# Moving the sums of gate blocks, the decay of the states and the products of decays from VectorE to GpSimd

## The chip, the cores and the metric

The kernel runs on one core of a Trainium2 chip. The metric is the device time of one execution in microseconds (us). A core has a matrix engine (TensorE, PE in the profile; its weight loads are PEld), a vector engine (VectorE, DVE), an activation engine (ScalarE, ACT), GpSimd (POOL), and a queue engine that only issues transfers (SyncE, SP). Each works through its own queue in order, and semaphores tie the queues together. Operands lie in SBUF (128 partitions); matmul results land in PSUM.

## What is computed

A gated linear recurrence over 768 tokens for 4 x 8 heads of 48 dimensions, followed by a two-layer network with a per-channel leaky activation, on 3072 tokens:

```python
f = 1.0 / (1.0 + np.exp(-f_logit))
for t in range(S):
    state = f[:, :, t, :, None] * state + np.einsum('bhd,bhe->bhde', k[:, :, t], v[:, :, t])
    y[:, :, t] = np.einsum('bhd,bhde->bhe', q[:, :, t], state)
...
x = attn_out.transpose(0, 2, 1, 3).reshape(B * S, H * D)     # 3072 x 384
h = x @ w_in                                                 # 384 x 2048
g = np.maximum(h, 0.0) + alpha * np.minimum(h, 0.0)
return g @ w_out                                             # 2048 x 384
```

Everything is float32.

## The kernel before

The recurrence is worked in chunks. A step handles two batch rows and 128 tokens; there are 12 steps (`steps`, L726), which alternate between the two pairs of batch rows, so that a step continues the state of the step two before it. Each step has four stages, written as generators that give up control after each piece: `prepare` (P, L258), `carry` (O, L432), `attend` (S, L506) and `network` (n, L609). The string `USUAL` (L37) lays out by hand in which order the pieces of neighbouring steps are issued; the order holds for TensorE, VectorE and ScalarE (L734). For GpSimd's and SyncE's queues there is no hand-written order: the framework's scheduler places their instructions by when their inputs and buffers are ready, and every queue then runs in the order that was built. In the steady state one period holds the recurrence of step n, the preparation of step n+1 and the network of step n-1.

`prepare` loads `f`, `q`, `k` and `v` (L266, L276; from step 1 on by GpSimd's queue), applies the sigmoid (L279) and forms products of gates: scans over 32-token blocks (`ps` L317, `ss` L319), scaled queries and keys (`us` L321, L330; `k4` L347; `kh`, `ks` L374, L398; `q3` L368, L406). Near its end it forms `f64`, the decay of the state over a half-chunk of 64 tokens, as a product of two entries of the scan `ps` (L414: four small multiplications of 48 x 8 elements in a middle step, whose input and output lie on different partitions).

`carry` makes the matmuls between blocks (`off`) and the new contribution to the state (`pd`, L484). The state lives in the free rows of the tile `vs`, beside the values. `moved(0)` at the end of `carry` and `moved(1)` in the last piece of `attend` bring it forward over a half-chunk: first the old state times `f64` (L494, 48 x 768), into the rows on the other side of the tile, then two additions of `pd` from PSUM (L498). `py` (L574) is the matmul that reads state and values; its result `y` is laid out as the network's input `xT` by ten transfers from the SP, ScalarE and GpSimd queues (L603).

`network` makes eight blocks of hidden units (`ph`, L618; 48 matmul calls into PSUM banks of a pool of four). ScalarE takes the negative part (L623), VectorE combines it to `gate` (L625). The second layer is not multiplied directly: it is done in seven block products instead of eight (`product`, L655 to L687), which needs four sums and differences of blocks of `gate`, the tile `S`, made by `sums` (L693) after the fourth and after the eighth `ph` block, 128 x 512 elements each. Of these S[1] needs S[0], and S[3] needs S[1]. The products run in the order `pa`, `pb`, then `pc` (reads S[1]), `pd` (S[0]), `pa` again, `pc` again (S[2]) and `pe` (S[3]). VectorE's additions after them (`plus`, L661) combine the results and so free the PSUM banks for the next network's `ph`. The first step's network is plain and has no sums, so 11 networks have them.

Of the kernel before, what the change touches and what calls it, by code (L numbers as in the profile page):

```python
# [15 lines left out]
ALU = mybir.AluOpType  # L16
# [5 lines left out]
U = 2  # L22
# [36 lines left out]
def kernel(  # L59
# [30 lines left out]
    nc = tc.nc  # L90
    B, NC, _, HP, _ = qT.shape
    DM = v.shape[-1]
    H = 2 * HP
    D = DM // H
# [27 lines left out]
    def pair(name):  # L122
        return psa.tile([128, 2, 512], F32, tag="pair", name=name)
# [124 lines left out]
    def rows(par):  # L248
        return slice(64 * par, 64 * par + D)
# [4 lines left out]
    def halves(cc):  # L254

        return slice(CH * cc, CH * cc + CH), slice(CH * (1 - cc), CH * (1 - cc) + D)

    def prepare(bp, c, x):  # L258
# [150 lines left out]
        f64 = x["f64"] = work.tile([128, U, H], F32, tag="f64", name=f"f64_{i}")  # L409
        by64 = pre.rearrange("p (a c j) i -> p a c j i", c=NC2, j=2)  # L410
        for cc in range(0 if c else 1, NC2 if c < NC - 1 else 1):
            for par in range(2):
                g64 = by64[rows(par), :, cc, :, NB]
                nc.vector.tensor_tensor(f64[halves(cc)[1], :, par:H:2].rearrange("p u h -> p (u h)"),  # L414
                                        g64[:, :, 0], g64[:, :, 1], ALU.mult)
        yield
        for cc in range(0 if c else 1, NC2):
# [14 lines left out]
    def carry(bp, c, x):  # L432

        i = f"{bp}_{c}"
        q3, ks, kh, f64 = (x[n] for n in ("q3", "ks", "kh", "f64"))
        off = pair(f"off_{i}")
        for u in range(U):
            for hp in range(HP):
                for cc in range(NC2):
                    g = (u * HP + hp) * NC2 + cc  # L440
                    o = (u * HP + hp) * DB
                    for par in range(2):
                        r_ = rows(par)
                        nc.tensor.matmul(off[CH * cc:CH * cc + DB, par, o:o + DB],  # L444
                                         lhsT=kh[r_, g], rhs=q3[r_, g, 2], start=True, stop=True)
        if not c:
            for u in range(U):
                for hp in range(HP):
                    for j in range(NJ):
                        g = (u * HP + hp) * NJ + j  # L450
                        o = U * HP * DB + (u * HP + hp) * 16
                        for par in range(2):
                            r_ = rows(par)
                            nc.tensor.matmul(off[DB * j:DB * (j + 1), par, o:o + 16], lhsT=x["k16"][r_, g],
                                             rhs=x["q16"][r_, g], start=True, stop=True)
            for u in range(U):
                o = U * HP * DB + u * HP * 16
                nc.scalar.copy(ad[:, u, :, :, 16:DB], off[:, :, o:o + HP * 16].rearrange("p r (h t) -> p r h t", h=HP))
        for cc in range(NC2):
            s_ = slice(CH * cc, CH * cc + DB)  # L460
            for par in range(2):
                nc.scalar.copy(A[s_, :, par * HP:(par + 1) * HP, CH * cc + DB:CH * (cc + 1)],
                               off[s_, par, 0:U * HP * DB].rearrange("p (u h t) -> p u h t", u=U, h=HP))


        if not c:
            pk = pair(f"pk_{i}")
            for u in range(U):
                for hp in range(HP):
                    a = (u * HP + hp) * NC2  # L470
                    nc.tensor.transpose(pk[:, u, hp * 128:(hp + 1) * 128], ks[:, a:a + 2].rearrange("p c s t -> p (c s t)"), ident)
            ksn = x["ksn"] = work.tile([128, U, HP * 128], F32, tag="ksn", name=f"ksn_{i}", bufs=1)
            for u in range(U):
                nc.scalar.copy(ksn[:, u], pk[:, u])
        yield
        pd = pair(f"pd_{i}")
        ksn = x["ksn"]
        for u in range(U):
            for hp in range(HP):
                for cc in range(NC2):  # L480
                    for par in range(2):
                        o = (u * HP + hp) * D
                        s_ = halves(cc)[0]
                        nc.tensor.matmul(pd[rows(par), cc, o:o + D],  # L484
                                         lhsT=ksn[s_, u, hp * 128 + 64 * par:hp * 128 + 64 * par + D],
                                         rhs=vs[bp][s_, cc, u, (2 * hp + par) * D:(2 * hp + par + 1) * D], start=True, stop=True)

        def moved(cc):

            of, to = halves(cc)[1], halves(1 - cc)[1]  # L490
            was, then = (vs[bp][p, a, :, 0:DM].rearrange("p u (h e) -> p u h e", e=D)
                         for p, a in ((of, cc), (to, 1 - cc)))
            if c or cc:
                nc.vector.tensor_tensor(then, was, f64[of].unsqueeze(3).broadcast_to((D, U, H, D)), ALU.mult)  # L494
            for par in range(2):
                now = pd[rows(par), cc, 0:U * HP * D].rearrange("p (u h e) -> p u h e", u=U, e=D)
                if c or cc:
                    nc.vector.tensor_tensor(then[:, :, par:H:2], then[:, :, par:H:2], now, ALU.add)  # L498
                else:
                    nc.scalar.copy(then[:, :, par:H:2], now)  # L500

        x["moved"] = moved
        moved(0)
        yield

# [103 lines left out]
    def network(bp, c, x):  # L609
# [3 lines left out]
        for f in range(NH):  # L613
            ph = bank(f"ph{f}_{i}")
            tiles = (2 * f, 2 * f + 1) if plain else (f, f + NH)
            for kt in range(NK):
                for j, m in enumerate(tiles):
                    nc.tensor.matmul(ph[:, j * T:(j + 1) * T], lhsT=w_in_sb[:, kt, m * 128:(m + 1) * 128],  # L618
                                     rhs=xT[:, kt], start=(kt == 0 and j == 0), stop=(kt == NK - 1 and j == 1),
                                     skip_group_check=True)  # L620
            neg = work.tile([128, 2, T], F32, tag="neg", name=f"neg{f}_{i}")
            phv = ph.rearrange("p (j t) -> p j t", j=2)
            nc.scalar.activation(neg, phv, AF.Relu, scale=-1.0)  # L623
            for j, m in enumerate(tiles):
                nc.vector.scalar_tensor_tensor(gate[:, m % NH, m // NH], neg[:, j], om[:, m:m + 1], phv[:, j],  # L625
                                               ALU.mult, ALU.add)
            if not plain and f % 4 == 3:
                sums(slice(f - 3, f + 1))
            yield
# [63 lines left out]
    def sums(fs_):  # L693

        s = late["S"]
        u0, u1 = slice(0, C), slice(C, T)
        of = lambda j, u: gate[:, fs_, j, u]
        for to, x_, y_, op in ((s[:, 0, fs_], of(0, u1), of(1, u1), ALU.add),
                               (s[:, 1, fs_], s[:, 0, fs_], of(0, u0), ALU.subtract),
                               (s[:, 2, fs_], of(0, u0), of(0, u1), ALU.subtract),  # L700
                               (s[:, 3, fs_], of(1, u0), s[:, 1, fs_], ALU.subtract)):
            nc.vector.tensor_tensor(to, x_, y_, op)  # L702

    def halves_of_w_out():

# [28 lines left out]
    with tc.manual_schedule(engines={mybir.EngineType.PE, mybir.EngineType.DVE, mybir.EngineType.Activation}):  # L734
        for _ in range(IDLE):
            nc.tensor.matmul(idle[0:32, 0:8], lhsT=ones[:, 0:32], rhs=ones[:, 0:8], start=True, stop=True)
        run = {}
        for n, step in enumerate(steps):
            x = {}
            for key, stage_ in zip("POSn", (prepare, carry, attend, network)):  # L740
                run[key, n] = stage_(*step, x)
        for key in order:
            next(run[key] if key in run else pieces[key[0]])
# [55 lines left out]
```

## Time and profile before

| | |
|---|---|
| median of 3 runs | 622.16 us (620.33 to 623.74) |
| span of the profiled execution | 622.1 us |
| VectorE, sums L702 | 88 instructions, 60.6 us, mean 688 ns |
| VectorE, decay of the states L494 | 20 instructions, 19.1 us, mean 952 ns |
| VectorE, products of decays L414 | 40 instructions, 6.7 us, mean 168 ns |
| VectorE, additions to the states L498 | 40 instructions, 22.1 us, mean 552 ns |
| GpSimd, issuing transfers (L266, L276, L603) | 77 instructions, 49.4 us |

The profiled execution's span is that of a median run. In the profile a group of instructions is named by its line, its engine and by tiles as output<-input (`S<-gate`); `us` as a tile name is a tile, not a unit. "Busy" counts an engine's instructions from start to end; instructions that follow each other closely overlap a little, so start-to-start distances are somewhat shorter than durations. A bracket such as `[0.17 <-DVE o L661]` gives the idle time ahead of an instruction and what ended it. A wait that is ended by several engines is put down to the one that came last. TensorE is told apart as matmul (PE) and weight load (PEld). What GpSimd has to do before the change is filling tiles at the start and issuing transfers; as its queue runs in order, a transfer that waits for its buffer holds up what stands behind it.

### The profile page before, as it was taken

The page shows a single profiled execution, that of the slowest core. Times are in us where ns is not written, and L with a number is a line of the kernel's source. Part 1 is how long each engine was busy: PE and PEld are TensorE (multiplying, and loading weights), DVE is VectorE, ACT ScalarE, POOL GpSimd, SP SyncE. Part 2 cuts the span into 40 slices and gives each one's busy share as a digit, 9 for nine tenths or more (in the row PEclk, how much of TensorE's full clock was granted, in tenths as well). Part 3 has the DMA queues.
Part 4 walks back from the last instruction along what each step waited for, and adds up shares of the span by engine and source line. Part 5 has one row for each costly group of instructions (what it writes and reads, how often), then busy time and mean ns, then how long its engine had stood idle before and what let it go on. Part 6 is the DMA issues. An engine that isn't in the chain of part 4 may idle for free.

```text
span 622.1 us, 19062 instructions
## 1 busy us (share of the span) xinstructions
PE 592.1 (95%) x8212; PEld 529.8 (85%) x8212; DVE 497.1 (80%) x997; ACT 246.6 (40%) x466; POOL 63.0 (10%) x117
## 2 busy tenths in 40 slices
PE   3568999999999999999999999999999999999997
PEld 3457866898899899899899899899889889889997
DVE  7588998899898798798798798798888888762261
ACT  5677862441641272262261351352253243223110
POOL 9120010001000011001001001001001000000000
PEclk9999999999999999999999999999999999999999
DMA  9964632014404314214313313413313401201000
GB/s 290 367 234 155 190 85 52 36 36 108 98 8 96 72 35 107 67 35 95 79 35 90 84 35 88 86 36 86 87 36 85 87 3 26 53 2 27 26 0 26
DMA packets 68116, 50.43 MB, mean 81 GB/s; under 512 B 47168, under 2 KB 60608, under 8 KB 68032
## 3 DMA queue, kind: packets, MB, share of 16 engines
q1 hardware_dynamic: 56656, 25.01, 15.6%
q0 software_dynamic: 6864, 22.35, 12.7%
q10 hardware_dynamic: 4512, 1.85, 1.7%
q8 instruction: 65, 1.06, 0.7%
q14 instruction: 19, 0.16, 0.1%
HBM read 36.21 MB, written 4.72 MB: 66 GB/s over the span
## 4 chain that ended last, share of the span: by engine, by line
PE 88%; DVE 6%; ACT 3%; issue 2%; DMA 1%; ACTq 0%; DVEq 0%
PE ph L618 39%; PE pc L657 9%; PE pa L657 8%; PE pd L657 5%; PE pe L657 4%; PE pb L657 4%; PE py L574 4%; PE po L638 3%; PE raw L520 3%; PE qu L535 3%; PE pd L484 3%; PE off L444 1%; PE xt L592 1%; DVE gate L625 1%; DMA f<-in_fT 1%
## 5 line engine op out<-in xcount | busy, mean ns | idle before, releaser
L618 PE MATMUL ph<-xT,w_in_sb 128*128 128x256 f32 x1152 | 258.7, 382 | 0.7 <-DVE Csum L661 0.7
L618 PEld LDWEIGHTS ph<-xT,w_in_sb 128*128 128x128 f32 x1152 | 216.4, 190 | 33.4 <-issue 2.3
L623 ACT ACTIVATE neg<-ph 128x512 f32<-128x512 f32 x96 | 57.4, 598 | 200.8 <-PE ph L618 139.5
L625 DVE SCALAR_TENSOR_TENSOR gate<-neg,om,ph 128x256 f32<-128x256 f32 x192 | 82.7, 478 | 50.6 <-ACT neg L623 50.4
L657 PE MATMUL pc<-t,S 128*128 128x192 f32 x352 | 61.7, 329 | 0.0
L657 PE MATMUL pa<-w_out_sb,gate 128*128 128x192 f32 x352 | 61.3, 327 | 0.1
L657 PEld LDWEIGHTS pa<-w_out_sb,gate 128*128 128x128 f32 x352 | 57.9, 190 | 1.0 <-DVE gate L625 0.4
L657 PEld LDWEIGHTS pc<-t,S 128*128 128x128 f32 x352 | 57.3, 190 | 0.6
L526 DVE COPY_PREDICATED ad<-mraw,raw 128x256 f32<-128x256 int32 (+1 forms) x96 | 42.4, 442 | 11.1 <-PE raw L520 8.6
L541 DVE COPY_PREDICATED ad<-mquad,qu 128x224 f32<-128x224 int32 (+6 forms) x140 | 42.0, 300 | 6.2
L419 ACT COPY A<-q 48x512 f32<-48x512 f32 x44 | 27.2, 619 | 36.1 <-DVE q L368 35.7
L563 ACT COPY A<-ad 32x256 f32<-32x256 f32 x96 | 38.7, 403 | 1.4
L330 DVE TENSOR_TENSOR us<-us,fs 128x768 f32<-128x768 f32 (+5 forms) x60 | 36.8, 614 | 0.0
L678 ACT ACTIVATE o<-pa 128x192 f32<-128x192 f32 x11 | 3.7, 332 | 75.2 <-PE pa L657 72.3
L661 DVE SCALAR_TENSOR_TENSOR Csum<-pc,Csum 128x192 f32<-128x192 f32 x22 | 7.9, 357 | 30.3 <-PE pc L657 30.1
L287 DVE TENSOR_TENSOR qd<-qd,f 128x768 f32<-128x768 f32 (+2 forms) x36 | 27.2, 756 | 6.0 <-ACT qd L282 6.0
L520 PEld LDWEIGHTS raw<-qd,k 48*32 48x32 f32 x1536 | 18.5, 109 | 15.3 <-issue 13.1
L520 PE MATMUL raw<-qd,k 48*32 48x80 f32 x1536 | 24.0, 243 | 7.6 <-issue 4.4
L702 DVE TENSOR_TENSOR S<-gate 128x512 f32<-128x512 f32 x44 | 30.3, 688 | 0.8
L657 PE MATMUL pe<-w_out_sb,S 128*128 128x192 f32 x176 | 30.4, 326 | 0.0
L657 PE MATMUL pd<-w_out_sb,S 128*128 128x192 f32 x176 | 30.4, 326 | 0.0
L657 PE MATMUL pb<-t,gate 128*128 128x192 f32 x176 | 30.4, 326 | 0.0
(101 smaller groups left out, 758.3 us busy)
## 6 DMA issues: line engine op xcount, KB each, us to landing
w_out_raw<-in_w_out SPq DMA_DIRECT2D x8, 767.8 KB, 5.8
w_in_raw<-in_w_in SPq DMA_DIRECT2D x8, 767.2 KB, 11.9
q<-in_qT POOLq DMA_DIRECT2D x11, 512.0 KB, 4.2
f<-in_fT POOLq DMA_DIRECT2D x11, 512.0 KB, 4.5
k<-in_kT POOLq DMA_DIRECT2D x11, 512.0 KB, 4.9
out<-o SPq DMA_DIRECT2D x24, 192.0 KB, 2.7
vs<-in_v POOLq DMA_DIRECT2D x22, 192.0 KB, 4.6
ksn<-kt SPq DMA_DIRECT2D x80, 32.0 KB, 2.0
```

The costliest lines, as they stand in the source:

```text
L287: nc.vector.tensor_tensor(qdv[d], qdv[d - 1][:, :, :, 1:5 - d], f[:, :, 1:5 - d].rearrange("p (g i) r -> p g i r", i=NB), ALU.mult)
L330: nc.vector.tensor_tensor(us[:, :, UO[m]:UO[m] + 4 * n].rearrange("p g (i r) -> p g i r", r=4), us[:, :, skip:skip + 4 * n].rearrange("p g ...
L419: nc.scalar.copy(A[halves(cc)[1], :, par * HP:(par + 1) * HP, CH * cc:CH * (cc + 1)], q3[rows(par)].rearrange("p (u h c) s t -> p u h c (s ...
L520: nc.tensor.matmul(raw[DB * j:DB * (j + 1), par, hp * C:hp * C + QW], lhsT=k[r_, g * DB:(g + 1) * DB], rhs=qd[r_, g], start=True, stop=True)
L526: nc.vector.copy_predicated(adu[:, :, :, d:4], mraw[:, d, :, d:4].bitcast(I32).unsqueeze(1).broadcast_to((128, H, NB, n)), rv[:, :, QO[d]: ...
L541: nc.vector.copy_predicated(ad[:, u, :, :, 4 * m:DB], mquad[:, lo:lo + n].bitcast(I32).unsqueeze(1).unsqueeze(1).broadcast_to((128, 2, HP, ...
L563: nc.scalar.copy(A[s_, u, :, s_], ad[s_, u].rearrange("p r h t -> p (r h) t"))
L618: nc.tensor.matmul(ph[:, j * T:(j + 1) * T], lhsT=w_in_sb[:, kt, m * 128:(m + 1) * 128], rhs=xT[:, kt], start=(kt == 0 and j == 0), stop=( ...
L623: nc.scalar.activation(neg, phv, AF.Relu, scale=-1.0)
L625: nc.vector.scalar_tensor_tensor(gate[:, m % NH, m // NH], neg[:, j], om[:, m:m + 1], phv[:, j], ALU.mult, ALU.add)
L657: nc.tensor.matmul(to[:, 0:DH], lhsT=of(f), rhs=by(f), start=(f == 0 and not more), stop=(f == NH - 1), skip_group_check=True)
L702: nc.vector.tensor_tensor(to, x_, y_, op)
```

## The change

Three calls move from VectorE to GpSimd, with the same operands:

```diff
@@ prepare
             for par in range(2):
                 g64 = by64[rows(par), :, cc, :, NB]
-                nc.vector.tensor_tensor(f64[halves(cc)[1], :, par:H:2].rearrange("p u h -> p (u h)"),
+                nc.gpsimd.tensor_tensor(f64[halves(cc)[1], :, par:H:2].rearrange("p u h -> p (u h)"),
                                         g64[:, :, 0], g64[:, :, 1], ALU.mult)
@@ carry, moved
             if c or cc:
-                nc.vector.tensor_tensor(then, was, f64[of].unsqueeze(3).broadcast_to((D, U, H, D)), ALU.mult)
+                nc.gpsimd.tensor_tensor(then, was, f64[of].unsqueeze(3).broadcast_to((D, U, H, D)), ALU.mult)
@@ sums
                                (s[:, 3, fs_], of(1, u0), s[:, 1, fs_], ALU.subtract)):
-            nc.vector.tensor_tensor(to, x_, y_, op)
+            nc.gpsimd.tensor_tensor(to, x_, y_, op)
```

VectorE keeps the gates, the additions to the states and all the rest of `prepare`. GpSimd now also runs, in a middle step, eight sums, two decays and four products beside its transfers; the products feed the decays on the same engine, the decays feed VectorE's additions, and the sums feed TensorE.

## The prediction, made before the changed kernel was run

> **What bounds the kernel now.** I read the page first, then one window per step of the steady part, then VectorE's timeline at the end of one step, then the waits.
>
> ```profile
> PE 592.1 (95%) x8212; PEld 529.8 (85%) x8212; DVE 497.1 (80%) x997; ACT 246.6 (40%) x466; POOL 63.0 (10%) x117
> ...
> PE 88%; DVE 6%; ACT 3%; issue 2%; DMA 1%; ACTq 0%; DVEq 0%
> ```
>
> TensorE (PE) is busy 95% of the span and makes 88% of the chain that ended last. VectorE (DVE) is busy 80%, GpSimd (POOL) 10%. The next view cuts the span at the first `raw` matmul of each step; columns are the stretch, its length, then busy us and instructions of each engine.
>
> ```profile
> 198.12:245.80 47.68, 47.61 (x658) 43.34 (x657) 40.21 (x79) 15.68 (x33) 4.47 (x7) 1.00 0.28 66
> 293.48:341.23 47.75, 47.65 (x658) 43.40 (x657) 41.45 (x86) 17.91 (x36) 4.47 (x7) 1.00 0.28 68
> ```
>
> In a step TensorE is without work for 0.1 us or less, at full clock. So freeing VectorE can give almost nothing in the ten steps that make up the time after 150 us; it can only lose, where VectorE becomes late for TensorE. The waits say where that is nearest (columns: us in total, times, longest):
>
> ```profile
> PEld ph L618 <- DVE Csum L661: 1.0, 1, 1.0
> PEld ph L618 <- DVE o L661: 0.9, 5, 0.2
> PEld pa L657 <- DVE gate L625: 0.4, 1, 0.4
> ```
>
> At five step ends (245, 293, 341, 388 and 436 us) the first `ph` load of the next network stands 0.17 us behind VectorE's `o` additions (L661), which free the PSUM banks; at 152 us 0.98 us. There VectorE has no slack. At 484 us the additions end 0.5 us ahead of that load, at 198 us 2.2 us. VectorE's timeline into the end of one such step (start, duration):
>
> ```profile
> 227.00 0.69 DVE L702 TENSOR_TENSOR S<-gate 128x512 f32<-128x512 f32 x1
> 227.72 0.69 DVE L702 TENSOR_TENSOR S<-S,gate 128x512 f32<-128x512 f32 x1
> ...
> 229.54 0.75 DVE L317 TENSOR_TENSOR_SCAN ps<-fs,ones 128x289 f32<-128x289 f32 x1
> ...
> 235.58 0.36 DVE L661 SCALAR_TENSOR_TENSOR Csum<-pc,Csum 128x192 f32<-128x192 f32 x1 [1.52 <-PE pc L657]
> ...
> 239.56 0.95 DVE L494 TENSOR_TENSOR vs<-vs,f 48x768 f32<-48x768 f32 x1
> 240.55 1.12 DVE L498 TENSOR_TENSOR vs<-vs,pd 48x384 f32<-48x384 f32 x2
> ...
> 245.66 0.72 DVE L414 TENSOR_TENSOR f<-ps 48x8 f32<-48x8 f32 x4
> 246.41 0.36 DVE L661 SCALAR_TENSOR_TENSOR Csum<-pc,Csum 128x192 f32<-128x192 f32 x1
> ```
>
> From the second group of sums (227.00) to the last additions (247.42) VectorE stands still once, 1.52 us for `pc`. All three moved kinds of work lie in this stretch, and its length decides.
>
> **The change: what VectorE loses.** L702: 88 instructions, mean 688 ns, 60.6 us. L494: 20 of 952 ns, 19.1 us. L414: 40 of 168 ns, 6.7 us. Together 86.4 us of 497.1. In the stretch, start to start: four sums 2.54 us (227.00 to 229.54), one decay 0.99 (239.56 to 240.55), four products 0.75 (245.66 to 246.41): 4.28 us. The other halves lie elsewhere: the first group of sums and the first decay at 214 to 217.8 us, ahead of places where VectorE waits for ScalarE anyway (0.68 us before L287, 0.31 us before the last gate). Removing them is worth nothing to TensorE, which covers them.
>
> **What GpSimd gains, and its price.** The trace has no two-input operation on GpSimd. From below: its memset of 512 elements, 0.53 us. From above: its affine select of 128 elements, 0.742 us, or 5.8 ns an element, which is 3.0 us for 512. I take a fixed 0.15 us (its 4-element copies last 0.178) and twice the memset's 0.88 ns an element (1.812 us for 2048), once per input: p = 0.15 + 512 x 1.76 ns = 1.05 us for a sum, 1.5 us for a decay of 768 elements, 0.2 us for a product. It is nearer the low end because a memset streams like a tensor operation and a select computes a condition. GpSimd's own load is no bound: 8 x 1.05 + 2 x 1.5 + 4 x 0.2 = 12.2 us on top of 4.47 in a step of 47.7. The Trainium skill (GPSIMD Engine Reference, 3.1) has 4497 ns for a two-input add of 2048 elements; an estimate from it is 1.12 us for a sum, by which the stretch below would be 0.3 us longer. No run here shows it.
>
> **Do the two engines hold each other up?** The start of the trace has GpSimd copies beside VectorE operations with two SBUF inputs:
>
> ```profile
> 7.31 0.18 POOL L166 COPY mquad<-inq 128x4 f32<-128x4 f32 x1
> ...
> 7.57 0.92 POOL L174 COPY mhalf<-inq 128x8 f32<-128x8 f32 x1
> ...
> 12.16 1.03 POOL L190 COPY dense<-ident 128x48 f32<-128x48 f32 x1
> ```
>
> A copy of 4 elements takes 0.18 us while VectorE is idle. The copy of 8 begun at 7.57 ends at 8.49, as VectorE's L287 (7.49 to 8.45) ends; the one begun at 12.16 ends at 13.19, as L321 (11.91 to 13.10) ends. A GpSimd read waits for the VectorE operation under way and gets in before the next. Whether VectorE then waits for GpSimd these short copies can't show: from below nothing, from above the whole GpSimd operation. I take a hold of most of it, as exclusion seen from one side is likely to work from both. The Trainium skill (SBUF — State Buffer, Who interferes with whom) says so: VectorE with two SBUF inputs and a GpSimd operation that reads SBUF share one read interface, and the second to come is blocked until the first ends. On GpSimd's side the trace agrees (1.03 us against 0.18); by the full rule the time would be about 632 us.
>
> **The sum.** GpSimd in the stretch: 4 x 1.05 + 1.5 + 4 x 0.2 = 6.5 us. If all of it holds VectorE, which loses 4.28 us of work and can use up the 1.52 us of idleness, the additions end 6.5 - 4.28 - 1.52 = 0.7 us later. Nine turns of the hold also lose the 0.09 us by which VectorE's operations overlap (0.69 long, 0.60 apart): 0.8 more. Against this, 2.9 us of the 13.6 us of other work (L661, L498, the transpose) read PSUM or one tensor and can run beside GpSimd; they lie behind 235.58, where GpSimd has the decay and products left, 2.3 us, so a fifth of that comes back: 0.4 us. I take +1.1 us a step end. Bounds: 4.28 us less work with no hold leaves -1.7 us (worth at most the 0.17 us wait); p = 3.0 us with a full hold gives 12 + 4.4 + 0.8 - 5.8, +11 us, which I count among the less than 1 in 10 above the range since no streaming row is near it. TensorE pays in full at the six step ends without slack, 0.6 at 484 us, nothing at 198 and 531 us: 6 x 1.1 + 0.6 = 7.2 us. Ramp and tail: nothing; the last network's `pc` starts at 605.8 and its second sum would end at 602.2 + 0.2 + 2 x 1.05 = 604.5. Sum on the profiled execution's 622.1 us, which is also the median (622.16): 629.3, say **629 us**; 625 to 637 for this case alone, from 0.5 to 2.2 us a step end.
>
> **New waits and queues.** GpSimd takes its queue in order:
>
> ```profile
> 206.54 0.73 POOL L266 DMA_DIRECT2D k<-in_kT  x1 [18.45 <-PE raw L520]
> 221.31 0.73 POOL L266 DMA_DIRECT2D q<-in_qT  x1 [14.04 <-ACT qd L282]
> 232.36 0.72 POOL L266 DMA_DIRECT2D f<-in_fT  x1 [10.32 <-DVE us L321]
> 233.08 0.61 POOL L276 DMA_DIRECT2D vs<-in_v  x1
> 234.08 1.08 POOL L603 DMA_DIRECT2D xT<-y  x2 [0.40 <-ACT y L583]
> ```
>
> The sums of 214 us have 7 us ahead of `q`. Those of 227 us end about 235, with VectorE's operations between them; `s2`, the first that TensorE reads, about 230.5 against `pc` at 232.7. The `f` and `vs` loads are for two steps on. The two `xT` transfers, behind sums, products and decay, go at about 239 instead of 234 and land 4.1 us later, 243 against `ph` at 247.6: covered, with 4 us to spare. The additions L498 now wait on VectorE for GpSimd's decay; queued behind them stand the gates at 217 us, and at 240 us the end of the stretch.
>
> **The rivals.** (a) *No hold*: GpSimd fits its reads into the gaps and VectorE isn't delayed; the step ends stay where they are, 621 to 622 us. For it: the VectorE operations beside the waiting copies kept their length (L287 0.96 us, as in its mean). (b) *L498 waits*: the first decay stands behind the first sums on GpSimd, 214.1 + 4 x 1.05 + 1.5 = 219.8, so the additions end 2 us later than 218.9; 1 us of that is swallowed by the idle 0.68 + 0.31, the last gate comes 1 us late where `pa` has 0.7 us, and the hold comes on top: some 2.3 us x 9 steps, 643 us. Against it: the decay's inputs are ready near 198 us, when GpSimd is idle. (c) *Faster*: the stretch gets shorter by up to 1.7 us and the waits of TensorE for VectorE go: 1.0 + 0.9 + 0.4 above, 0.2 for L526, and 2 x 0.35 us of L414 in the ramp at 19.9 and 50.3 us, 3.2 us: 619 us. It decides if a sum holds VectorE for less than 0.5 us; against it stands that the whole pool is hardly 3 us.
>
> **How the numbers follow.** Forecast 0.50, (b) 0.15, (a) 0.26, (c) 0.09. A measurement tells about 0.5%, 3.1 us, from no change; so slower 0.65, same 0.26, faster 0.09. The range 618.5 to 643 takes in (c) and most of (b), and leaves larger prices of p out.
>
> **What would show it.** Right: L702, L494, L414 on GpSimd, sums of 1 to 1.3 us apart; L317 to L347 each begun later than the one before ended, or longer, while sums run; `Csum` after `pc` at or past its old distance; PEld `ph` waiting 1 us or more for L661 at six step ends, steps of 48.8 us instead of 47.7. Wrong: steps of 47.7 us with VectorE idle more, rival (a); waits of L498 for GpSimd, rival (b); `pc` waiting for `S` or `ph` for `xT` would show a GpSimd queue that I have ordered wrongly.

## The result, and the profile after

The changed kernel takes 632.22 us (median of 4, 630.29 to 633.9) against 621.86 us before (median of 4): a ratio of 1.0165, 95% interval 1.0136 to 1.0195. It is slower by some 10 us.

The page of the changed kernel, engines and the chain that ended last:

```profile
PE 592.1 (94%) x8212; PEld 527.7 (84%) x8212; DVE 463.0 (73%) x849; ACT 246.1 (39%) x466; POOL 254.6 (40%) x265
...
PE 68%; DVE 13%; POOL 7%; issue 5%; ACT 5%; DMA 1%; ACTq 0%; DVEq 0%
```

VectorE gave up 86.4 us of work, yet is busy only 34.1 us less: the other 52 us are its remaining operations, which got longer. GpSimd, whose operations were no part of the chain, now has 7% of it. Two steps, cut at the first `raw` matmul as before:

```profile
202.45:250.97 48.52, 47.73 (x657) 43.16 (x656) 36.66 (x70) 17.29 (x35) 21.85 (x21) 1.00 0.27 66
250.97:299.61 48.64, 47.70 (x658) 43.15 (x657) 37.68 (x72) 17.86 (x35) 21.86 (x21) 1.00 0.28 67
```

TensorE's busy time in a step is what it was, 47.7 us; the step is 0.9 us longer. The waits of its weight loads after the start show for what (us in total, times, longest):

```profile
PEld pc L657 <- POOL S L702: 7.6, 7, 1.8
...
PEld ph L618 <- DVE o L661: 1.0, 6, 0.2
PEld pc L657 <- DVE Csum L661: 1.0, 1, 1.0
```

The product `pc` waits seven times for the sums on GpSimd. The wait for L661 at the step ends, which the forecast saw growing to more than 1 us, is still 0.17 us each. GpSimd's timeline in one step:

```profile
230.87 2.96 POOL L702 TENSOR_TENSOR S<-gate 128x512 f32<-128x512 f32 x2 [4.62 <-DVE gate L625]
233.91 3.77 POOL L414 TENSOR_TENSOR f<-ps 48x8 f32<-48x8 f32 x4
237.76 1.26 POOL L702 TENSOR_TENSOR S<-S,gate 128x512 f32<-128x512 f32 x1
239.10 1.47 POOL L494 TENSOR_TENSOR vs<-vs,f 48x768 f32<-48x768 f32 x1
```

The queue was built in another order than the source's: S[0] and S[2], then the four products of decays, and only then S[1], which `pc` reads. The products are 48 x 8 elements, but 0.94 us each. S[1] ends at 239.02. The second half of `pc`, which reads blocks 4 to 7, could have started at 238.1:

```profile
236.79 1.27 PEld L657 LDWEIGHTS pc<-t,S 128*128 128x128 f32 x8
239.07 1.27 PEld L657 LDWEIGHTS pc<-t,S 128*128 128x128 f32 x8 [1.01 <-POOL S L702]
```

VectorE's timeline at the same place:

```profile
231.09 1.68 DVE L317 TENSOR_TENSOR_SCAN ps<-fs,ones 128x289 f32<-128x289 f32 x1
232.69 1.76 DVE L319 TENSOR_TENSOR_SCAN ss<-fs,ones 128x289 f32<-128x289 f32 x1
234.37 1.19 DVE L321 TENSOR_TENSOR us<-us,f 128x1024 f32<-128x1024 f32 x1
...
240.76 0.36 DVE L661 SCALAR_TENSOR_TENSOR Csum<-pc,Csum 128x192 f32<-128x192 f32 x1 [3.15 <-PE pc L657]
```

The scan L317 took 0.75 us before and 1.68 now: VectorE is held for 0.93 us by a sum that lasts 1.27. L321, beside a product, keeps its length; there the product waits. VectorE stands 3.15 us for `pc` where it stood 1.52: 1.0 us of the difference is `pc`, which itself waits for GpSimd, and by the rest VectorE comes earlier than before. Counted from the start of `py` (234.71 us here, 230.51 before), it ends L330 at 2.9 us instead of 3.55.

### The profile page after: what moved, and what is told of

The parts are those of the page before. It is cut to its first block, busy times and chain, and to the rows that moved or that the text cites. A ratio compares the mean times of both kernels' runs of the same rounds, so it can differ in the third digit from the quotient of the medians.

```text
span 630.4 us, 19095 instructions
## 1 busy us (share of the span) xinstructions
PE 592.1 (94%) x8212; PEld 527.7 (84%) x8212; DVE 463.0 (73%) x849; ACT 246.1 (39%) x466; POOL 254.6 (40%) x265
## 4 chain that ended last, share of the span: by engine, by line
PE 68%; DVE 13%; POOL 7%; issue 5%; ACT 5%; DMA 1%; ACTq 0%; DVEq 0%
PE ph L618 30%; PE pc L657 8%; PE pa L657 6%; PE pe L657 5%; POOL S L702 4%; PE pd L657 4%; PE po L638 3%; PE raw L520 3%; POOL f L414 3%; PE qu L535 3%; DVE qd L287 3%; DVE gate L625 2%; PE py L574 2%; PE pb L657 2%; PE pd L484 1%
## 5 line engine op out<-in xcount | busy, mean ns | idle before, releaser
L625 DVE SCALAR_TENSOR_TENSOR gate<-neg,om,ph 128x256 f32<-128x256 f32 x192 | 82.6, 476 | 74.9 <-ACT neg L623 74.8
L702 POOL TENSOR_TENSOR S<-gate 128x512 f32<-128x512 f32 x44 | 60.5, 1394 | 155.7 <-DVE gate L625 155.7
L266 POOL DMA_DIRECT2D k<-in_kT x11 | 8.0, 731 | 155.9 <-PE raw L520 155.9
L657 PE MATMUL pc<-t,S 128*128 128x192 f32 x352 | 63.7, 331 | 6.2 <-POOL S L702 5.5
L330 DVE TENSOR_TENSOR us<-us,fs 128x768 f32<-128x768 f32 (+5 forms) x60 | 47.1, 785 | 0.0
L414 POOL TENSOR_TENSOR f<-ps 48x8 f32<-48x8 f32 x40 | 33.3, 832 | 17.8 <-DVE ps L317 10.5
L661 DVE SCALAR_TENSOR_TENSOR Csum<-pc,Csum 128x192 f32<-128x192 f32 x22 | 7.8, 353 | 42.8 <-PE pc L657 42.7
L494 POOL TENSOR_TENSOR vs<-vs,f 48x768 f32<-48x768 f32 x20 | 36.2, 1812 | 1.3
L702 POOL TENSOR_TENSOR S<-S,gate 128x512 f32<-128x512 f32 x22 | 31.7, 1441 | 1.7
L702 POOL TENSOR_TENSOR S<-gate,S 128x512 f32<-128x512 f32 x22 | 30.6, 1390 | 1.7
```

Of the source, the lines that this page charges most:

```text
L330: nc.vector.tensor_tensor(us[:, :, UO[m]:UO[m] + 4 * n].rearrange("p g (i r) -> p g i r", r=4), us[:, :, skip:skip + 4 * n].rearrange("p g ...
L414: nc.gpsimd.tensor_tensor(f64[halves(cc)[1], :, par:H:2].rearrange("p u h -> p (u h)"), g64[:, :, 0], g64[:, :, 1], ALU.mult)
L494: nc.gpsimd.tensor_tensor(then, was, f64[of].unsqueeze(3).broadcast_to((D, U, H, D)), ALU.mult)
L657: nc.tensor.matmul(to[:, 0:DH], lhsT=of(f), rhs=by(f), start=(f == 0 and not more), stop=(f == NH - 1), skip_group_check=True)
L702: nc.gpsimd.tensor_tensor(to, x_, y_, op)
```

## The experiments

**One part at a time.** Four kernels put a part of the change on GpSimd and leave the rest on VectorE. Each edit is a choice among the change's three lines, here the first:

```diff
-nc.vector.tensor_tensor(then, was, f64[of].unsqueeze(3).broadcast_to((D, U, H, D)), ALU.mult)
+nc.gpsimd.tensor_tensor(then, was, f64[of].unsqueeze(3).broadcast_to((D, U, H, D)), ALU.mult)
...
-            nc.vector.tensor_tensor(to, x_, y_, op)
+            nc.gpsimd.tensor_tensor(to, x_, y_, op)
```

Sums and decays, without the products:

> Sums and decays on GpSimd, the four products of decays (L414) back on VectorE. In the built queue of GpSimd the sum S[1] then follows S[0] and S[2] directly instead of standing behind the four products. Theory A (queue order: TensorE's pc waits for S[1], which stands behind products that last 0.83 us each because each waits for a VectorE operation): pc's waits for S, 7.6 us at seven step ends, go but for 1 to 2 us near 138 us; time 623 to 625 us. Theory B (the forecast: GpSimd's reads hold VectorE, whose additions L661 are late at the step ends): GpSimd still holds VectorE by 4 x 1.27 + 1.5 us against 3.5 us taken from it, so ph waits 0.5 to 1 us for L661 at six step ends; time 627 to 631 us.

Sums alone (the second of the two edits above):

> Only the sums (L702) on GpSimd. Theory A: S[1] follows S[0] and S[2] directly, no wait of pc after 145 us; 621 to 624 us. Theory B: the sums take 5.1 us of GpSimd where VectorE gives up 2.54 us and has 1.52 us of idleness, so the step ends come about 1 us later, 6 or 7 times: 627 to 630 us.

Products and decays, without the sums:

> Products and decays on GpSimd, sums on VectorE. Theory A: nothing waits for S on GpSimd; 621 to 623 us. Theory B: in the stretch VectorE gives up 1.7 us; products and decays hold it for 2 to 3 us, step ends up to 1 us late: 623 to 629 us. If the time is some 2 us above the span, as in the changed kernel, what lies outside the span comes from arithmetic on GpSimd of any of the three kinds.

Products alone:

> Only the four products of decays a step (L414) on GpSimd; sums and decays on VectorE, as before. Theory A and B: nothing of S waits, little is held: 621 to 623 us both. The products should last 0.2 us where VectorE reads one tensor and 0.7 to 1.3 us beside its operations with two SBUF inputs. If the time is 624 us or more, neither theory holds, and the loss comes from where the products move the transfers in GpSimd's queue.

| on GpSimd | median us | ratio to before, 95% interval |
|---|---|---|
| sums, decays, products (the change) | 632.22 | 1.0165 [1.0136, 1.0195] |
| sums, decays | 627.28 | 1.0096 [1.0074, 1.0118] |
| sums | 627.97 | 1.0098 [1.0083, 1.0112] |
| decays, products | 623.22 | 1.0021 [1.0007, 1.0035] |
| products | 621.25 | 1.0000 [0.9982, 1.0019] |

Neither theory alone accounts for the first of the four parts, sums and decays. Both limits can be seen there, in the waits of TensorE's weight loads:

```profile
PEld ph L618 <- DVE Csum L661: 4.8, 7, 0.9
...
PEld pc L657 <- POOL S L702: 1.8, 1, 1.8
```

The six waits of `pc` of about 1 us are gone, as theory A has it; but now `ph` waits for VectorE at seven step ends, 0.82 to 0.86 us at five of them, which is theory B. VectorE is late there because the four products, back on it, take 1.94 us instead of 0.72 beside a decay. They start 15.28 us after `py`, and 15.15 before, so that up to them VectorE is only 0.13 us later (VectorE first, then GpSimd):

```profile
245.56 1.94 DVE L414 TENSOR_TENSOR f<-ps 48x8 f32<-48x8 f32 x4
```

```profile
246.00 1.47 POOL L494 TENSOR_TENSOR vs<-vs,f 48x768 f32<-48x768 f32 x1 [8.02 <-DVE f L414]
```

With sums alone, theory B has no step-end wait to show (0.17 us five times, as before). Four holds of 0.93 to 1.07 us are just the 2.54 us of sums that VectorE gave up and its 1.52 us of idleness. The loss lies in one place, near 140 us, where `pc` waits 4.8 us, once:

```profile
PEld pc L657 <- POOL S L702: 4.8, 1, 4.8
```

```profile
139.85 2.93 PE L657 MATMUL pc<-t,S 128*128 128x192 f32 x8 [4.46 <-POOL S L702]
```

Behind the wait TensorE is also slower for a moment: the granted clock is 0.69 from 139 to 141 us and 0.50 from 141 to 143 us in this trace, and this half of `pc` and the `pd` behind it take 1.7 us more than in the run below with the first sums on VectorE. Together that is the 6.5 us. GpSimd and VectorE of that place:

```profile
134.23 5.57 POOL L702 TENSOR_TENSOR S<-S,gate 128x512 f32<-128x512 f32 x1
```

```profile
134.15 0.75 DVE L317 TENSOR_TENSOR_SCAN ps<-fs,ones 128x289 f32<-128x289 f32 x1
134.82 0.73 DVE L319 TENSOR_TENSOR_SCAN ss<-fs,ones 128x289 f32<-128x289 f32 x1
135.47 1.20 DVE L321 TENSOR_TENSOR us<-us,f 128x1024 f32<-128x1024 f32 x1
136.59 1.22 DVE L347 TENSOR_TENSOR k<-k,kr 128x1024 f32<-128x1024 f32 x1
137.72 0.95 DVE L330 TENSOR_TENSOR us<-us,fs 128x768 f32<-128x768 f32 x1
```

Here the sum begins 0.08 us after the start of a VectorE operation (L317) and gets no turn until a run of five has ended, 1.1 us before its own end. None of the five got longer.

The last two rows need less. With decays and products the median is 1.75 us above before, and theory A had up to 623 us; its trace (an execution of 621.97 us) has no longer waits than before from 60 us on, so where that time lies is not shown. With products alone nothing is lost, as expected, though some products last up to 3.75 us, more than the 1.3 that was expected of them.

**The kernel before, again, and the two places apart.** The kernel before as it is:

> The kernel before, unchanged, for a second trace with its own time. If the time outside the span is 1.6 to 1.9 us here too, GpSimd's arithmetic adds nothing there, and the first trace of before (span 622.1 us) belongs to an execution of about 623.8 us, slower than the median: the changed kernel's loss is then read too small from the two traces. Expected: 621.5 us, span 619.5 to 620.5 us, the difference to the first trace in the first 85 us.

It took 621.3 us, ratio 0.9995 [0.9983, 1.0008]. The profiled execution took 622.01 us with a span of 620.2, so 1.8 us lie outside the span without any arithmetic on GpSimd. In the changed kernel it is 632.2 against 630.4. The first trace of before, with its span of 622.1 us, therefore belongs to an execution of about 623.9 us and not to the median (the highest on record there took 623.74). Losses are counted against this second trace from here on.

Sums alone, but with the first network's left on VectorE:

```diff
-                sums(slice(f - 3, f + 1))
+                sums(slice(f - 3, f + 1), nc.vector if (bp, c) == steps[1] else nc.gpsimd)
...
-            nc.gpsimd.tensor_tensor(to, x_, y_, op)
+            eng.tensor_tensor(to, x_, y_, op)
```

> Sums alone on GpSimd, but those of the first network that has any on VectorE. In the run with all sums on GpSimd, pc waited 4.8 us once, near 140 us, for a sum that stood behind five VectorE operations in a row, and nowhere else. If that one place is the whole loss of that run (628.0 against 621.5 us): 621 to 623 us. If the sums' hold on VectorE costs something in every step as well, as the forecast has it: 624 us or more. A gain below 620 us would make it the better version; expected at most 1 us, from steps of 47.6 instead of 47.7 us.

It took 621.2 us, ratio 0.9998 [0.9985, 1.001]. So the one place was the whole loss of sums alone (627.97). The other ten networks' sums on GpSimd cost nothing that can be measured, and give nothing either, though VectorE has 55.1 us fewer of its own to do.

All three kinds, with the products kept behind the sums in GpSimd's queue:

```diff
-                nc.gpsimd.tensor_tensor(f64[halves(cc)[1], :, par:H:2].rearrange("p u h -> p (u h)"),
-                                        g64[:, :, 0], g64[:, :, 1], ALU.mult)
+                with tc.issue_after(late["sum"].ins) if "sum" in late else ExitStack():
+                    nc.gpsimd.tensor_tensor(f64[halves(cc)[1], :, par:H:2].rearrange("p u h -> p (u h)"),
+                                            g64[:, :, 0], g64[:, :, 1], ALU.mult)
...
-            nc.gpsimd.tensor_tensor(to, x_, y_, op)
+            late["sum"] = nc.gpsimd.tensor_tensor(to, x_, y_, op)
```

> All three kinds on GpSimd, as in the change, but the four products kept behind the sums in GpSimd's queue. Theory A (the loss is pc waiting for S[1], which stands behind the products): six waits of about 1 us go; 625 to 627 us, with about 2 us left near 138 us. Theory C (two limits, the second hidden by the first: with S[1] early, VectorE's additions L661 become late at the step ends, held by sums, products and decays): pc's waits go and ph waits 0.7 to 1.2 us for L661 at six step ends instead; 628 to 633 us. A third way: xT goes behind all of this at some 243 us in the step and lands near 247, so that ph waits for a transfer.

It took 625.15 us, ratio 1.0071 [1.0051, 1.0092], as theory A has it. The waits (lines of the kernel stand one further down here):

```profile
PEld pc L658 <- POOL S L703: 1.8, 1, 1.8
PEld ph L619 <- DVE Csum L662: 1.4, 6, 0.3
PEld pc L658 <- DVE Csum L662: 1.3, 1, 1.3
```

Putting the products behind the sums thus takes away 7 of the 10 us, though not all through `pc`: its waits for S are 5.8 us less, and `py` of the second step starts at 83.72 us instead of 85.94, ahead of the first sum (119 us). That part is the start, below. What theory C expected at the step ends stays small, 0.23 us each. Did VectorE not become late, then? It did:

```profile
228.50 1.68 DVE L317 TENSOR_TENSOR_SCAN ps<-fs,ones 128x289 f32<-128x289 f32 x1
230.10 1.76 DVE L319 TENSOR_TENSOR_SCAN ss<-fs,ones 128x289 f32<-128x289 f32 x1
231.78 2.23 DVE L321 TENSOR_TENSOR us<-us,f 128x1024 f32<-128x1024 f32 x1
233.93 2.29 DVE L347 TENSOR_TENSOR k<-k,kr 128x1024 f32<-128x1024 f32 x1
```

The third of the last additions ends 17.64 us after the start of `py` in this run (249.76 - 232.12) and 16.91 before (247.42 - 230.51), 0.73 us later. In between, six of VectorE's operations are longer than before by 6.6 us in all. But in this build `ph` takes a bank that the addition `Csum` frees, 0.66 us ahead of the one that it waited for before; so 0.06 us of 0.73 is paid.

**The two places together, and the start.** Products behind the sums, and the first network's sums on VectorE:

> All three kinds on GpSimd, the products kept behind the sums in its queue, and the sums of the first network that has any on VectorE: the two places where pc waits for S are both taken away. If these two are the loss: 621.5 to 623.5 us, with 1.3 us left near 190 us, where pc waits for VectorE's Csum. If the hold on VectorE at the step ends costs what the forecast said (1.1 us at six of them): 627 us or more.

It took 623.49 us, ratio 1.0046 [1.0029, 1.0064], at the upper end of what was expected. From 230 us on its steps are as long as before (333.4 us from one `py` to that seven steps later, before 333.6); what is left is the `pc` wait for `Csum` near 190 us and a start that varies.

The change, again:

> The change, unchanged, for a second trace: is the start up to the first py near 84 us, where the first trace lost 2.5 us against the second trace of before (TensorE 3.6 us without an instruction at 51.5 us, granted clock 0.66 from 50 to 60 us), lost in every execution or by chance? If by chance: span 627 to 629 us in an execution with py near 83.5 us. If the four products and the decay between the early transfers cause it: again 85 us or more, and time 631 to 633 us. The waits of pc for S near 138 us (1.8) and in six steps (about 1 us each) should stand as before in either case.

It took 631.27 us, ratio 1.0151 [1.0133, 1.017]; `py` at 85.91 us, the same waits of `pc`, 7.6 us. So the two traces of the change agree on the start. That it is lost in every execution doesn't follow: both traces are of executions above 632 us, and two of the four here took 629.21 and 630.08 us (spans of 627.4 and 628.3), near what was expected without this loss. TensorE in the start of the changed kernel (first trace):

```profile
55.12 0.68 PE L454 MATMUL off<-us 48*32 48x16 f32 x46 [3.57 <-issue]
```

The change with the products and decays of the first two steps on VectorE:

```diff
-                nc.gpsimd.tensor_tensor(f64[halves(cc)[1], ...
+                (nc.gpsimd if c else nc.vector).tensor_tensor(f64[halves(cc)[1], ...
...
-                nc.gpsimd.tensor_tensor(then, was, ...
+                (nc.gpsimd if c else nc.vector).tensor_tensor(then, was, ...
```

> The change, but in the first two steps products and decay on VectorE, as before; from the third step on nothing differs. In both traces of the change TensorE stands 3.6 us near 51.5 us, and a transfer of instructions lies between 51 and 56 us, among the loads of f, v and w_out, where the other traces have it before 51 us. If GpSimd's products and decay, which put the loads of v and f off from 42.1 and 43.9 to 45.6 and 46.2 us, cause this: that wait falls below 1 us, py comes near 83.5 instead of 85.9 us, and the time is 628.5 to 629.5 us. If they don't: 631 to 632.5 us, and the start stays open. pc's waits for S, 7.6 us, stand in either case.

It took 628.9 us, ratio 1.0125 [1.0097, 1.0153], in the range that was expected (one of six executions took 632.6). `py` starts at 82.27 us, earlier than expected; the wait at L454 is 1.05 us, and `pc`'s waits for S are unchanged. So in this build, putting the six small multiplications of the first two steps (four products, two decays) back on VectorE gains 2 to 3 us.

They don't cost that in every build, and the later loads alone don't explain it. Three other runs have the same six on GpSimd (decays and products; products behind the sums; the two places together), and with decays and products the loads of `v` and `f` go as late (45.3 and 45.9 us against 45.6 and 46.2). The `py` of their second step starts at 83.96, 83.72 and 84.05 us, against 83.47 in the second trace of before and 84.87 in the first.

What goes with the loss is a transfer of instructions. TensorE stops at this same instruction of L454 in all twelve traces, for 0.42 to 3.69 us, waits for nothing else that the profile shows, and goes on 2.2 to 2.8 us after such a transfer has begun: at 55.12 after 52.70 in the change, at 51.30 after 48.86 in the last run, at 52.41 after 50.22 and at 54.35 after 51.58 in the two traces of before. In ten traces this transfer begins before the second of two weight loads (`w_out_raw`, issued between 47 and 53 us), in both traces of the change some 3 us after it. That TensorE waits for its own instructions is thus the likeliest reading, but no run moved that transfer alone, and why it comes late only in the change stays open.

## Why the prediction was right, and where it wasn't

The forecast was slower, 629 us; 632.2 us lies in the range and the direction is right. Its mechanism is half of the truth, and that its sum came near is in part luck: what it missed replaced what it counted.

- *TensorE is the bound, and VectorE's lost work buys nothing*: right. No version was faster than before by more than the interval of its measurement, and steps without waits stay at 47.6 us.
- *Price of GpSimd's operations*: 1.27 us for a sum instead of 1.05, 1.47 for a decay alone instead of 1.5; a sum is 2.2 ns an element after the 0.15 us, and so much nearer to twice the memset's 0.88 than to the select's 5.8. A product lasts 0.22 us alone, as taken, but 0.83 in the median, since each waits for a VectorE operation: this wait was seen in the copies at the start, and not put into the price.
- *The hold*: right. L317 and L319 are held by 0.93 and 1.03 us of a sum's 1.27, while the gates (L625), which read PSUM, keep their length (0.47 us beside an operation of GpSimd, 0.48 otherwise). With the products behind the sums the hold is 6.6 us in a stretch, where the forecast had 6.5 if all of GpSimd's time there holds. The Trainium skill's rule (SBUF — State Buffer, Who interferes with whom), that the second to come is blocked until the first ends, agrees with these; the sum that waited 5.57 us goes beyond it, as it sat out five operations. That the forecast's 632 us by the full rule are the measured figure is luck: they come from lateness at the step ends, which cost nothing here. That a GpSimd read gets in before VectorE's next operation, as the forecast read from two copies, is thus not always so.
- *The sum, +1.1 us a step end*: mis-sized. With all three kinds and an early S[1] it is 0.73 us, of which 0.06 us is paid, as the additions free the banks one after the other and `ph` may take an earlier one. In the change itself it isn't paid at all: the last `Csum` starts 1.18 us later after `py` than before, but 0.98 of that is there from the step's first `Csum` on, as `pc` comes late for TensorE and VectorE alike. With sums and decays alone 0.7 us more than before is paid, for the products that are back on VectorE.
- *The step that failed* is the one on new waits and queues: "`s2`, the first that TensorE reads, about 230.5 against `pc` at 232.7". Counted from `py` as before, S[1] came at 234.8 and not 230.5. It assumed that the four sums stand together in GpSimd's queue and gave the products no place among them. In the built queue S[2] and the four products stand ahead, 1.7 + 3.8 us. The forecast named `pc` waiting for S as the sign of this.
- *Ramp: nothing*: wrong by 2.5 us in the traces (`py` at 83.47 us in the second of before, 85.94 and 85.91 in the change). The last run takes this away; its cause is open.
- *The profiled execution is the median*: wrong. It was an execution 1.8 us above its span and some 2 us above the median.

Where the 10.2 us between the spans (620.2 and 630.4) are, by the start of `py` in the two traces: 2.5 up to 84 us; 2.6 between 84 and 143 us, where `pc` waits 1.8 us for S and `pa` longer for the gates, beside VectorE operations that the first sums hold; 1.0 gained at 152 us, where the old wait for `Csum` is gone, as rival (c) had it; 1.7 between 185 and 235 us, a wait of `pc` for `Csum` and one for S; 4.5 in the next five steps, 0.9 each, by `pc`'s wait for S[1]. After that only two products stand ahead of S[1], and then none, and the steps lose nothing.

Rival (b), L498 waiting for the decay, didn't come about: L498 waits for `pd` only. Rival (c)'s gain was real but 1.0 us. Rival (a), no hold, fell with L317.

## What to carry to other kernels

Work moved to an engine whose queue a scheduler orders must be read in the built queue, not in the source: what counts is what stands ahead of the one result that the bounding engine reads next, and a tiny operation there can cost a large one's wait. Two engines that hold each other up don't add their capacities; taking 86 us from VectorE left it only 34 us less busy. Before crediting an engine with relief, ask if the bounding engine ever waits for it: here the waits of TensorE for VectorE were some 2.5 us in all.

## What the runs showed that was not expected

Who gets the turn between GpSimd and VectorE isn't even. Mostly they alternate, one operation each (L317 to L347 above). But a GpSimd operation that begins just after a VectorE operation of a close run can be shut out for the whole of it: a sum for 5.57 us (1.27 alone), a decay for 8.52 us in the run with sums and decays (1.47 alone), a product for 3.7 us in three runs (0.22 alone). What decides between the two was not found.
